# Attention and feed-forward on one core: folded weights stored in three transfers a tile, the third chunk's first unit loaded earlier, and folds, norms and global scores in other slots

## The chip, the cores and the metric

The kernel runs on one core of one Trainium2 chip. The metric is the time of one execution in device microseconds. The engines are TensorE (PE, with PEld for its weight loads), VectorE (DVE), ScalarE (ACT), GpSimd (POOL) and SyncE (SP), whose queue issues nearly all transfers (DMA).

## The reference, cut to what matters

Eight batches of eight heads: 512 local positions that attend to a window of 32 on each side and to 32 global ones, and 32 global positions that attend to everything. The result goes through an RMS norm and a gated feed-forward.

```python
s_ll = np.where(np.abs(pos[:, None] - pos[None, :]) <= 32, s_ll, -1e9)
out_l = sm(concat([s_lg, s_ll])) @ concat([v_g, v_l])     # local
out_g = sm(s_g) @ v_all                                   # global
xn = x / sqrt(mean(x * x) + 1e-6) * rms_g                 # x: 4608 x 512
return silu(xn @ w_gate) * (xn @ w_val) @ w_out           # 512 -> 1536 -> 512
```

## The kernel before

**Chunks and layers.** A chunk is the 512 local rows of one batch; chunk 8 is the 256 global rows of all. "Layer c" is the feed-forward of chunk c. While TensorE does layer c, the attention of chunk c+1 runs between its matmuls. Chunk 0, its layer and the attention of chunk 1 are written out by hand in a string `ORDER`, one token for each step (`J0 j0 u0`: the parts of fold 0; `o0`: a result of chunk 0; `U1.0` to `Y1.3`: the norm of chunk 1). Every step goes onto its engines' queues in the order of the program, and each queue runs in order.

**Slots.** From layer 1 on, one loop goes over the slots of a layer. Layer 1 has 72: 48 of products (`p`, six matmuls each, L1205) and 24 of outputs (`po`, L1266). Layers 2 to 7 are paired: seven products of halves take the place of eight, with sums and differences of weights, 42 slots of twelve matmuls (`pq`, L1108), then 24 of outputs. In each slot the program writes the slot's matmuls, then whatever attention steps are due, at most one with TensorE, then the evictions, then folds and fetches.

**Attention steps.** Chunk c has two local units, c.0 and c.1 (L loads q and k, V loads v, S the scores, M and N half a softmax each on VectorE, E and F the exponentials on ScalarE, D the division on GpSimd, T a transpose `et<-e` on VectorE, A and B the values `a<-et,v`, X and Y their eviction and squares), and from chunk 2 on a global unit between them (GL, GV loads, GS scores, GM, GN softmax, GT transposes, GA values, GD, GX). Each step names earlier steps and a distance in slots. `FIRST`, `UNIT` say from which slot a unit may begin, `LG` and `GG` hold distances: `LG[0]` is 4 slots from L to S in chunk 2, `GG[0]` 4 slots from GL to GS. A comes two slots behind the last of four T.

**Norms.** `NORM` and `NORMS` say how many slots before the end of a layer the norm of the next chunk is issued: squares, sums, all, and the halves (`ht`, `xh`, `xl`: high and low 16-bit parts that the first products of the next layer read).

**Folds.** For the paired layers the 12 weight tiles are folded once: `sums` adds high and low parts and makes four combinations in five VectorE additions (L1054 to L1058), `high` casts (ScalarE), `low` subtracts (VectorE, L155 through a helper), `store` writes the tile's quarters and combinations to a buffer `wd` in DRAM. Folds 0 to 2 stand in `ORDER`, fold 3+i in layer 1 at slots `FOLD*i`, +2, +3 and +5, with `FOLD` 8. `fetch` reads a pair's weights back for each paired layer (`wt<-wd`).

**Buffers.** The four banks `pa` of PSUM are shared by all attention steps and by the norm of chunk 1. Fold tiles, global keys, queries and values, and `ht` share six buffers `st`.

## Time and profile before

| | |
|---|---|
| median of 3 runs | 949.93 us (949.13 to 951.41) |
| the profiled execution | 949.54 us, its span 947.5 us |
| TensorE busy | 900.5 us, 95% of the span |
| VectorE, ScalarE, GpSimd busy | 635.3, 496.2, 254.2 us |
| mean granted TensorE clock | 0.980 |
| DMA queue 1 | 73824 packets, 171.41 MB, 54.8% of 16 engines |

Layer 1 begins at 170.9 us and layer 2 at 289.8; the paired layers that follow take about 100 us each; the last layer begins at 896.7. The profile lists for each engine how long it was busy, whom it waited for, and the granted clock of TensorE in any window.

### The profile page before, as it was taken

The page shows a single profiled execution, that of the slowest core. Times are in us where ns is not written, and L with a number is a line of the kernel's source. Part 1 is how long each engine was busy: PE and PEld are TensorE (multiplying, and loading weights), DVE is VectorE, ACT ScalarE, POOL GpSimd, SP SyncE. Part 2 cuts the span into 40 slices and gives each one's busy share as a digit, 9 for nine tenths or more (in the row PEclk, how much of TensorE's full clock was granted, in tenths as well). Part 3 has the DMA queues.
Part 4 walks back from the last instruction along what each step waited for, and adds up shares of the span by engine and source line. Part 5 has one row for each costly group of instructions (what it writes and reads, how often), then busy time and mean ns, then how long its engine had stood idle before and what let it go on. Part 6 is the DMA issues. An engine that isn't in the chain of part 4 may idle for free.

```text
span 947.5 us, 26480 instructions
## 1 busy us (share of the span) xinstructions
PE 900.5 (95%) x11028; PEld 615.5 (65%) x11028; DVE 635.3 (67%) x1603; ACT 496.2 (52%) x1232; POOL 254.2 (27%) x219
## 2 busy tenths in 40 slices
PE   6489899899998999999999999999999999999998
PEld 4344455544455886588747884688568865876584
DVE  6999987677767677656784679467756774655231
ACT  6999992444534573455553564357345732443131
POOL 0000000042323343323532353235333432233020
PEclk9699999999997999999999999999999999999999
DMA  9972430795449955195707762585438532787000
GB/s 351 406 277 87 158 117 2 239 266 158 147 150 312 290 184 194 48 301 192 245 36 218 250 211 108 165 283 180 159 123 300 182 102 86 234 266 236 34 1 22
DMA packets 74374, 173.41 MB, mean 183 GB/s; under 512 B 7568, under 2 KB 26256, under 8 KB 74256
## 3 DMA queue, kind: packets, MB, share of 16 engines
q1 hardware_dynamic: 73824, 171.41, 54.8%
q8 instruction: 86, 1.41, 0.6%
q10 hardware_dynamic: 432, 0.33, 0.1%
q14 instruction: 32, 0.26, 0.1%
HBM read 150.21 MB, written 21.50 MB: 181 GB/s over the span
## 4 chain that ended last, share of the span: by engine, by line
PE 80%; DMA 8%; DVE 7%; ACT 2%; issue 1%; SPq 1%; POOL 0%; ACTq 0%; DVEq 0%; POOLq 0%
PE pq L1108 35%; PE po L1266 22%; PE p L1205 9%; PE a L707 4%; PE po L1333 3%; PE s L664 3%; DMA k<-in_qk_dram 2%; DMA k<-in_qkb_dram 1%; DMA v<-in_vw_dram 1%; DMA wr<-in_w_in_dram 1%; DMA wt<-wd 1%; PE gs L780 1%; PE ga L837 1%; DMA gkq<-in_gkq_dram 1%; PE gt L823 1%
## 5 line engine op out<-in xcount | busy, mean ns | idle before, releaser
L1108 PEld LDWEIGHTS <-wt 128*128 128x128 f16 x3024 | 293.5, 98 | 46.0 <-issue 8.7
L1266 PE MATMUL po<-wo,h 128*128 128x512 f16 x1080 | 236.8, 379 | 0.5 <-POOL h L157 0.5
L1108 PE MATMUL pq<-xh,wt 128*128 128x256 f16 x1152 | 204.0, 274 | 0.5 <-issue 0.5
L1266 PEld LDWEIGHTS <-h 128*128 128x128 f16 x1080 | 105.0, 98 | 124.8 <-POOL h L157 1.0
L157 POOL TENSOR_TENSOR h<-t,h 128x512 f16<-128x512 f32 (+1 forms) x90 | 101.7, 1135 | 280.2 <-ACT h L1248 244.8
L1108 PE MATMUL pq<-ht,wt 128*128 128x256 f16 x1296 | 157.0, 273 | 3.9 <-DVE ht L155 2.1
L1108 PE MATMUL pq<-xl,wt 128*128 128x256 f16 x576 | 157.9, 274 | 0.0
L1205 PE MATMUL p<-xh,wf 128*128 128x512 f16 x384 | 120.4, 386 | 6.9 <-DVE t L1302 6.6
L1205 PEld LDWEIGHTS <-wf 128*128 128x128 f16 x576 | 56.2, 99 | 75.7 <-issue 14.4
L1140 POOL TENSOR_TENSOR s<-s,s 128x512 f32<-128x512 f32 x36 | 48.6, 1350 | 190.7 <-ACT s L1137 115.1
L626 ACT ACTIVATE e<-e,sm 128x128 f32<-128x128 f32 x192 | 75.1, 392 | 40.9 <-DVE sm L612 40.9
L641 POOL TENSOR_TENSOR e<-e,sm 128x512 f32<-128x512 f32 x48 | 50.2, 1047 | 124.5 <-DVE sm L640 121.4
L1170 ACT CAST h<-t 128x512 f16<-128x512 f32 x72 | 44.3, 616 | 58.6 <-DVE t L1162 58.0
L1162 DVE SCALAR_TENSOR_TENSOR t<-t,c_h,v 128x512 f32<-128x512 f32 x72 | 74.5, 1042 | 0.0
L1205 PE MATMUL p<-xl,wf 128*128 128x512 f16 x192 | 73.9, 385 | 0.0
L1126 DVE TENSOR_TENSOR v<-pq,s 128x512 f32<-128x512 f32 x72 | 49.6, 689 | 31.1 <-PE pq L1108 30.5
L1151 ACT ACTIVATE t<-u,half_inv 128x512 f32<-128x512 f32 x72 | 48.1, 715 | 27.6 <-DVE u L1126 19.4
L612 DVE CUSTOM_DVE_ANT_0 e<-s,maskb 128x128 f32<-128x128 f32 x192 | 45.8, 279 | 12.6 <-PE s L664 12.6
L1133 ACT COPY s<-pq 128x512 f32<-128x512 f32 x36 | 20.8, 578 | 63.2 <-PE pq L1108 63.1
L1139 DVE TENSOR_TENSOR s<-pq,s 128x512 f32<-128x512 f32 x36 | 24.8, 688 | 42.9 <-PE pq L1108 21.9
L1126 DVE TENSOR_TENSOR u<-pq,s 128x512 f32<-128x512 f32 x36 | 24.9, 692 | 38.9 <-PE pq L1108 15.4
L1158 DVE SCALAR_TENSOR_TENSOR t<-t,u 128x512 f32<-128x512 f32 x72 | 46.9, 680 | 0.0
(352 smaller groups left out, 1284.8 us busy)
## 6 DMA issues: line engine op xcount, KB each, us to landing
wt<-wd SPq DMA_DIRECT2D x114, 512.0 KB, 4.7
wr<-in_w_in_dram SPq DMA_DIRECT2D x24, 512.0 KB, 9.8
wt<-wd SPq DMA_DIRECT2D x48, 256.0 KB, 4.8
k<-in_qkb_dram SPq DMA_DIRECT2D x24, 448.0 KB, 6.2
gkq<-in_gkq_dram SPq DMA_DIRECT2D x16, 576.0 KB, 6.9
out_dram<-o SPq DMA_DIRECT2D x34, 256.0 KB, 2.0
v<-in_vb_dram SPq DMA_DIRECT2D x24, 352.0 KB, 7.2
v<-in_vw_dram SPq DMA_DIRECT2D x16, 512.0 KB, 9.6
```

Of the source, the lines that this page charges most:

```text
L157: nc.gpsimd.tensor_tensor(dst, a, b, ALU.subtract)
L612: nc.vector.tensor_tensor_reduce(out=e[:, g, :], in0=ps[:, g * P : (g + 1) * P], in1=late["mask"][:, m * P : (m + 1) * P], scale=-0.125, s ...
L626: nc.scalar.activation(e[:, g, :], e[:, g, :], AF.Exp, bias=sm[:, 0, j + g : j + g + 1], scale=-1.0, accum_out=sm[:, 1, j + g : j + g + 1],)
L641: nc.gpsimd.tensor_tensor(e, e, r.unsqueeze(2).to_broadcast([P, 4, P]), ALU.mult)
L1108: nc.tensor.matmul(ps[:, j * HT : (j + 1) * HT], w[:, j, i, k * P : (k + 1) * P], x[:, k * HT : (k + 1) * HT], start=first, stop=(p in end ...
L1126: nc.vector.tensor_tensor(o, ps, x.rearrange("p (j n) -> p j n", j=2), ALU.add)
L1140: nc.gpsimd.tensor_tensor(s(6), s(6), s(1), ALU.add)
L1151: nc.scalar.activation(t, st["u"][:, j, :], AF.Tanh, scale=half_inv[:, f : f + 1])
L1158: nc.vector.scalar_tensor_tensor(t, t, 1.0, u, ALU.add, ALU.mult)
L1162: nc.vector.scalar_tensor_tensor(t, t, c_h[:, f : f + 1], st["v"][:, j, :], ALU.mult, ALU.mult)
L1205: nc.tensor.matmul(ps[:, :n], rows[:, a, o : o + P], ch[z][k][:, :n], start=(k == 0 and i == 0), stop=(k == NK - 1 and i == 2),)
L1266: nc.tensor.matmul(ps[0], ch["h", f][:, a, j * P : (j + 1) * P], wo[f][:, z, :], start=(f == 0 and q == 0), stop=(f == NF - 1 and q == 2),)
```

## The change

1. A new step `G` in `ORDER`, ahead of fold 0, issues the loads of unit 2.0; its scores may follow in slot 0 of layer 1 (before: loads in slot 0, scores in slot 4).
2. `LG[0]` is no longer used: unit 2.1 has eight slots from L to S. `FIRST` lets global unit 0 begin at slot 14 and unit 2.1 at 22 (19 and 31).
3. `GG[0]`: six slots from a global unit's loads to its scores, in all layers.
4. `FOLD` 6: folds 3 to 11 begin at slots 0, 6, ... 48 (0, 8, ... 64).
5. `NORM`: the norm of chunk 2 is issued 4 to 5 slots earlier in layer 1, that of chunk 8 5, 7, 7 and 10 slots later in layer 7.
6. `wd` has another order of its eight parts, such that a fold is stored by three transfers and a pair's tile for a layer is fetched by one transfer in all cases, two of three full ones in two runs a partition.

```diff
-d16 A6 O2.0 X6 C7.0 C7.1 Q6 A7 a17 Z6 O2.1 X7 d17 Q7 O2.2 Z7 J0 j0 u0 O2.3 N1.0 N1.1 N1.2 N1.3
+d16 A6 O2.0 X6 C7.0 C7.1 Q6 A7 a17 Z6 O2.1 X7 d17 Q7 O2.2 Z7 G J0 j0 u0 O2.3 N1.0 N1.1 N1.2
...
-    GG = (4, 5, 4, 3)
-    NORM = {1: (16, 15, 13, 11)}
+    GG = (6, 5, 4, 3)
+    NORM = {1: (20, 19, 17, 16)}
     NORMS = (22, 21, 19, 17)
-    FIRST = (0, 19, 31)
+    FIRST = (0, 14, 22)
+    NORM[B - 1] = (17, 15, 12, 7)
-    FOLD = 8
+    FOLD = 6
...
-            ("S", scores, 1, [("L", LG[0] if c == EARLY else LG[1]), ("^Y", 1)]),
+            ("S", scores, 1, [("L", LG[1]), ("^Y", 1)]),
...
-            for q, o in ((0, 1), (1, 4), (3, 6), (2, 7)):
-                nc.sync.dma_start(to[:, o], wf[f][:, :, q * HT : (q + 1) * HT])
-            for q, o, n in ((0, 0, 1), (1, 2, 2), (3, 5, 1)):
-                nc.sync.dma_start(to[:, o : o + n], st["d"][:, q : q + n])
+            for a in range(2):
+                w = wf[f][:, a, :].rearrange("p (q n) -> p q n", q=4)
+                nc.sync.dma_start(to[:, 1::2, a, :], w)
+            nc.sync.dma_start(to[:, 0::2], st["d"])
...
-        ops = [(0, 2 * i, 2)] if i < 3 else [(0, 6, 1)]
+        o, d, n = ((0, 1, 2), (2, 2, 2), (3, 3, 2), (7, 1, 1))[i]
         if c == B:
-            ops = ([(0, 1, 1), (1, 4, 1)], [(0, 6, 2)])[i]
-        for to, o, n in ops:
-            nc.sync.dma_start(t[:, to : to + n], wd[g][:, o : o + n])
+            o, d, n = ((1, 2, 2), (5, 2, 2))[i]
+        nc.sync.dma_start(t[:, :n], wd[g][:, o : o + d * (n - 1) + 1 : d])
...
+    def first_loads():
+        for st in todo[:2]:
+            issue(st)
+            st["at"] = -LG[1]
+    job["G"] = first_loads
```

SP's queue at the end of chunk 0, before (`out_dram<-o`: the four results of chunk 0; `maskb` to `v`: the loads of unit 2.0):

```order
L1347 DMA out_dram<-o_2147 128x512
L1347 DMA out_dram<-o_2155 128x512
L1347 DMA out_dram<-o_2173 128x512
L1347 DMA out_dram<-o_2191 128x512
L586 DMA maskb<-in_maskb_dram 128x768
L587 DMA same<-in_eyes_dram 128x128
L591 DMA q_2217<-in_qkb_dram 128x512
L593 DMA k_2219<-in_qkb_dram 128x896
```

and now:

```order
L587 DMA maskb<-in_maskb_dram 128x768
L588 DMA same<-in_eyes_dram 128x128
L592 DMA q_2039<-in_qkb_dram 128x512
L594 DMA k_2041<-in_qkb_dram 128x896
L592 DMA q_2043<-in_qkb_dram 128x512
L594 DMA k_2045<-in_qkb_dram 128x896
L602 DMA v_2047<-in_vb_dram 128x704
L602 DMA v_2049<-in_vb_dram 128x704
L1347 DMA out_dram<-o_2162 128x512
L1347 DMA out_dram<-o_2170 128x512
L1347 DMA out_dram<-o_2188 128x512
L1347 DMA out_dram<-o_2206 128x512
```

The loads have moved in front of the four results.

VectorE in layer 1, ahead of the values of unit 2.1, before (`et<-e`: its last two transposes; `wq<-wf` and `ws`: the additions of fold 9; `t`: evictions of products):

```order
L646 STREAM_TRANSPOSE et_3010<-e_3086 128x512
L640 RECIPROCAL sm_2941<-sm_2941 128x4
L1236 SCALAR_TENSOR_TENSOR t_3164<-t_3164,p_11_3144 128x512
L646 STREAM_TRANSPOSE et_3011<-e_3123 128x512
L1245 SCALAR_TENSOR_TENSOR t_3164<-t_3164,c_h,p_11_3174 128x512
L1054 TENSOR_TENSOR wq_3206<-wf_1291 128x1024
L1055 TENSOR_TENSOR ws_3207<-wq_3206 128x256
```

and now (the additions are those of fold 10):

```order
L647 STREAM_TRANSPOSE et_2961<-e_3034 128x512
L641 RECIPROCAL sm_2892<-sm_2892 128x4
L1236 SCALAR_TENSOR_TENSOR t_3111<-t_3111,p_10_3091 128x512
L1054 TENSOR_TENSOR wq_3125<-wf_1335 128x1024
L1055 TENSOR_TENSOR ws_3126<-wq_3125 128x256
L1056 TENSOR_TENSOR ws_3126<-ws_3126,wq_3125 128x256
L1057 TENSOR_TENSOR ws_3126<-wq_3125 128x256
L1058 TENSOR_TENSOR ws_3126<-wq_3125,ws_3126 128x256
L647 STREAM_TRANSPOSE et_2962<-e_3071 128x512
```

The last transpose has moved behind a fold's additions.

VectorE at the end of layer 1, before (`h_2`, `ht`, `xl`: halves of the norm of chunk 2; `wq<-wf`, `ws`: fold 11; `sm`, the next row: softmax of unit 3.0):

```order
L999 TENSOR_TENSOR h_2_3595<-x_2_3336,x_0_2680 128x512
L1054 TENSOR_TENSOR wq_3598<-wf_1386 128x1024
L1055 TENSOR_TENSOR ws_3599<-wq_3598 128x256
L1056 TENSOR_TENSOR ws_3599<-ws_3599,wq_3598 128x256
L1057 TENSOR_TENSOR ws_3599<-wq_3598 128x256
L1058 TENSOR_TENSOR ws_3599<-wq_3598,ws_3599 128x256
L640 RECIPROCAL sm_3376<-sm_3376 128x4
L612 ISA e_3615,sm_3376<-s_3380,maskb 128x128
```

and now (`o`: a result of layer 1):

```order
L1000 TENSOR_TENSOR h_2_3504<-x_2_3289,x_0_2627 128x512
L1279 TENSOR_SCALAR o_3507<-po_3351,kk 128x512
L647 STREAM_TRANSPOSE et_3427<-e_3435 128x512
L641 RECIPROCAL sm_3358<-sm_3358 128x4
L613 ISA e_3533,sm_3358<-s_3360,maskb 128x128
```

Fold 11 has moved away from between `h_2` and `ht`, which is made from it.

## The prediction

> **What bounds the kernel now.** I read the page's first table and chain first, then TensorE's (PE's) waits, then the timeline of each engine around each wait. First the page: share of the span and, last, the chain by engine.

> ```profile
> PE 900.5 (95%) x11028; PEld 615.5 (65%) x11028; DVE 635.3 (67%) x1603; ACT 496.2 (52%) x1232; POOL 254.2 (27%) x219
> PE 80%; DMA 8%; DVE 7%; ACT 2%; issue 1%; SPq 1%; POOL 0%; ACTq 0%; DVEq 0%; POOLq 0%
> ```

> TensorE is busy 95% and carries 80% of the chain, and the change takes no matmul away. So only TensorE's waits can be won, and the matmuls that run on a lowered clock after a wait. This is who was waited for, by line (us in total, times, longest):

> ```profile
> PE s L664 <- DMA k<-in_qkb_dram: 3.3, 2, 2.0
> PE a L707 <- DVE et L646: 2.3, 1, 2.3
> PE pq L1108 <- DVE ht L155: 2.1, 1, 2.1
> PE a L707 <- issue: 1.9, 1, 1.9
> PE gs L780 <- DMA gkq<-in_gkq_dram: 1.7, 1, 1.7
> PE po L1266 <- POOL h L157: 0.5, 1, 0.5
> ```

> These six are 11.8 us of idle time, all at places that the change touches; the waits left out here lie nearly all in the first chunk, whose order it leaves alone. A slot, the unit in which the program places its steps, is six matmuls in layer 1 and twelve half as wide in a paired layer (chain rows):

> ```profile
> 373.39 1.30 PE po L1266 x6
> 331.66 1.31 PE pq L1108 x12
> ```

> **The change, part by part.** *Loads of unit 2.0 ahead of the results of chunk 0.* The sync queue (SP) issues in order, and its rows show why the first scores of layer 1 wait (start, duration):

> ```profile
> 146.71 1.10 PE L536 MATMUL a<-v,pt 128*32 128x64 f32 x64
> 168.40 3.64 SPq L1347 DMA_DIRECT2D out_dram<-o  x4
> 179.51 0.42 PE L664 MATMUL s<-k,q 64*32 64x128 f32 x8 [1.99 <-DMA k<-in_qkb_dram]
> 181.21 3.23 PE L664 MATMUL s<-k,q 64*32 64x128 f32 x120 [1.27 <-DMA k<-in_qkb_dram]
> ...
> 332.90 2.05 PE L664 MATMUL s<-k,q 64*32 64x128 f32 x128
> ```

> The four results of chunk 0 hold the loads back until 172.0, and the scores end at 184.44. TensorE had been free since 179.51 - 1.99 = 177.5, and undisturbed scores last 2.05 (layer 2's), so 6.9 - 2.0 = 4.9 us are lost. In the new order the loads wait only for their buffers, which the last values of chunk 0 free at 147.8, some 24 us before the scores, now in slot 0. Those need the four PSUM banks that the norm of chunk 1 has just used; VectorE (DVE) empties the last one here:

> ```profile
> 172.25 0.74 DVE L903 SCALAR_TENSOR_TENSOR xl<-x13t,gvec,xh 128x512 f16<-128x512 f32 x1
> ```

> It ends at 172.99; the scores would begin near 172.2 and come to that bank a microsecond later. Cost of the new wait: 0 to 0.8, I take 0.2. Gain 4.7. Behind it unit 2.0's softmax starts earlier beside fold 3, and its values stay 14 slots behind its scores (4 to 18 before, 0 to 14 now). I net that wait at 0, with -0.5 and +1.5 as ends.

> *Unit 2.1's loads 9 slots ahead of its scores instead of 4.* Its scores lasted 2.54 while the keys landed, against the 2.05 above: gain 0.5, at worst 0.

> ```profile
> 235.46 2.54 PE L664 MATMUL s<-k,q 64*32 64x128 f32 x128
> ```

> *Folds every 6 slots instead of 8.* This is the part that can cost. VectorE's busy time in the stretch of layer 1 up to unit 2.1's last values:

> ```profile
> 172.00:262.00 90.00, 64.41 (x161) 0.96 0.67 205
> ```

> By then seven of the nine folds are done; now it will be eight, some 4 us more (five additions at 2.72 by the starts below, a subtraction at 1.2). The stretch loses four slots of 1.30 and about 5 us of waits. So 68.5 us of work go into 80: 86% where it was 72%. At one place the order itself gets worse. Unit 2.1's last transpose (T3) stood ahead of a fold's additions, now it stands behind fold 10's. Before, on VectorE, and the values on TensorE:

> ```profile
> 244.53 1.22 DVE L1054 TENSOR_TENSOR wq<-wf 128x1024 f32<-128x1024 f16 x1
> 247.25 0.70 DVE L646 STREAM_TRANSPOSE et<-e 128x512 f32<-128x512 f32 x1
> ...
> 254.30 0.71 DVE L646 STREAM_TRANSPOSE et<-e 128x512 f32<-128x512 f32 x1 [0.40 <-POOL e L641]
> ...
> 256.28 1.54 PE L707 MATMUL a<-et,v 32*64 32x256 f32 x80
> ```

> A fold's additions hold VectorE from 244.53 to 247.25, 2.72 us. T3 ended at 255.0, 1.3 us before the values. It now ends 2.72 - 0.40 later (the wait for POOL is filled), and up to 0.8 more where POOL slows the additions or ACT starts later; the values stay 14 slots behind the scores. That is a new wait of 1.0 to 1.9, plus what VectorE is behind by. I take 2.0, with 0 and 2.8 as ends. Behind the waiting values stands only the next slot of products.

> Does such a wait also lower the clock? This window stands right behind the "issue" wait of 1.9 us (its numbers: length, busy, granted clock, DMA share, GB/s):

> ```profile
> 210.40:214.80 4.40, 4.40 (x17) 0.61 0.97 265
> ```

> 1.9 us idle was followed by 4.40 us at 0.61, a loss of 1.7. Behind the 1.7 us wait for gkq (below) the matmuls kept their pace. So the clock term for a wait of 2.0 is 0 or 1.7; I leave it at 0 and put 1.7 into the upper end. [...]

> *Folds and the norm out of the end of layer 1.* Around the change of layers TensorE waits twice, and VectorE is the reason:

> ```profile
> 287.62 1.22 DVE L1054 TENSOR_TENSOR wq<-wf 128x1024 f32<-128x1024 f16 x1
> 291.25 0.93 DVE L155 TENSOR_TENSOR ht<-h,ht 128x512 f16<-128x512 f32 x1
> 293.30 1.21 DVE L155 TENSOR_TENSOR wq<-ws,wq 128x1024 f16<-128x1024 f32 x1
> 296.54 0.70 DVE L646 STREAM_TRANSPOSE et<-e 128x512 f32<-128x512 f32 x1
> ...
> 292.23 1.70 PE L1108 MATMUL pq<-ht,wt 128*128 128x256 f16 x11 [2.13 <-DVE ht L155]
> 297.30 2.44 PE L707 MATMUL a<-et,v 32*64 32x256 f32 x78 [2.32 <-DVE et L646]
> ...
> 292.30:295.00 2.70, 2.67 (x13) 0.65 0.97 302
> 297.30:303.10 5.80, 5.80 (x95) 0.50 0.78 231
> ```

> Fold 11's additions (2.72) stand right ahead of ht's low half, its subtraction (1.2) ahead of T3 of unit 3.0, and VectorE has no gap there. Idle: 2.13 + 2.32. Slow clock: 2.70 x 0.35 + 5.80 x 0.50 = 0.9 + 2.9. Together 8.3. Now both last folds are over by slot 53, the norm starts 4 to 5 slots (5 to 6.5 us) earlier against a wait of 2.1, and unit 3.0's chain loses 2.72 + 2 x 1.2 of foreign work against a wait of 2.3. Both waits go, and with them the clock loss: gain 8.3. If one of them stays, half goes: 4.2.

> *Global units' scores 6 slots behind their loads instead of 4.* In layer 7 two scores wait for gkq; beside them an undisturbed one:

> ```profile
> 310.76 1.20 PE L780 MATMUL gs<-gkq 64*32 64x272 f32 x32
> 805.82 1.75 PE L780 MATMUL gs<-gkq 64*32 64x272 f32 x32
> 836.37 0.66 PE L780 MATMUL gs<-gkq 64*32 64x272 f32 x8
> 838.72 1.12 PE L780 MATMUL gs<-gkq 64*32 64x272 f32 x24 [1.69 <-DMA gkq<-in_gkq_dram]
> ```

> Lost: 0.6, and 839.84 - 836.37 - 1.1 = 2.4. Two slots of a paired layer are 2.6 us, so scores that would begin at 839.0 find the tile that landed at 838.7. Gain 3.0; 1.5 if it lands later. In layers 2 to 6 the transposed result (GX) moves behind the next unit's scores and takes the bank that the first two half softmaxes free; in layer 2 those end at 335.6, and TensorE gets there one slot behind the scores, at 334.95 + 1.31 = 336.3, so 0, at worst 0.6 in each of five layers.

> ```profile
> 335.34 0.28 DVE L612 CUSTOM_DVE_ANT_0 e<-s,maskb 128x128 f32<-128x128 f32 x1
> ```

> *The last norm later.* Its POOL additions kept h back for the 0.5 us of the last wait listed above: gain 0.5. It now ends 7 slots (9.1 us) later than here, and it was ready 17 us before the last layer's products:

> ```profile
> 878.34 0.75 DVE L155 TENSOR_TENSOR xl<-xg,xh 128x256 f16<-128x256 f32 x2
> 896.72 31.44 PE p L1205 x288
> ```

> *Three store transfers instead of seven, strided fetches.* Same bytes in the same runs of 512 B and 1 KB; fetches in two runs instead of one. SP issues three transfers where it issued seven, of the same rows in all, so it is busy no longer than before. No TensorE row waits for wt or for a store, so 0 on the path. The cover is that a fold's buffer is needed again 7 slots (9.1 us) behind its store; stores land in 4.0 us (last number, a median).

> ```profile
> wd<-wf SPq DMA_DIRECT2D x48, 128.0 KB, 4.0
> ```

> *The "issue" wait* of 1.9 (3.6 with its slow clock) has no cause that the profile names. It fell among small matmuls, and the DMA share right behind it is 0.97. The new order puts the same values two slots behind the loads of the same global unit, so I keep it: 0, with 3.6 gained or a second one of 3.6 as ends.

> **Sum.** -4.7 - 0.5 + 0 + 2.0 - 8.3 - 3.0 - 0.5 + 0 = -15.0. The profiled execution took 949.54 (span 947.5, 2.0 around it), 0.04% under the median of 949.93. 949.54 - 15.0 = 934.5.

> **The rivals.** (a) The "issue" wait goes too: 934.5 - 3.6 = 930.9. For it: the loads of unit 2.0 leave the crowded start of layer 1. Against: the stores there are as many.

> (b) VectorE becomes the bound of layer 1. At 86% it falls behind, unit 2.0's values wait 1.5, unit 2.1's 2.8 with a clock loss of 1.7, and its scores 0.8 for the bank that GD frees behind fold 8: 1.5 + 0.8 + 1.7 + 0.8 = 4.8 more, 939.3. For it: T3's place. Against: in the stretch up to 262 no TensorE row waits for VectorE today.

> (c) One wait between layers 1 and 2 stays, because unit 3.0's chain still has the same 17 slots: 934.5 + 4.2 = 938.7.

> (d) Slower: the stores of three transfers land too late. Folds 8, 10 and 11 reuse a tile whose store was issued 7 slots (9.1 us) earlier. What lands later holds VectorE, and at 86% that goes on to TensorE, three times. To end above 951.4 it needs 16.9 us, 5.6 each: landing after 14.7 us, against 4.0 above. (e) No change: the loads are not early, because SP stands still, and VectorE's waits come back elsewhere: 949.

> **Numbers.** Forecast 0.45, own range 932 to 937.5; (a) 0.22, (b) 0.16, (c) 0.09, (d) 0.05, (e) 0.03. A measurement of this kernel can tell about 0.2% (1.9 us) from no change. Faster holds all but the last two: 0.92; same 0.03; slower 0.05. The range of 928 to 941 takes in (a) to (c) with some 2 us around them; it leaves out (d), (e) and mixtures of (b) with (c).

> **What would show it.** Right: scores of unit 2.0 undisturbed near 172 to 174.4; no wait and a granted clock of 1.00 at the start of layer 2; gs of 1.1 in layer 7; a wait of a L707 for et of about 2 us near 240. Wrong: PE waits in layer 1 for VectorE of more than 4 us, a clock below 1 there, or VectorE waiting for a DMA at L1054.

## The result, and the profile after

The new kernel takes 934.77 us, the one before 949.53 (medians of six runs each). The ratio is 0.9845, 95% interval 0.982 to 0.987: 14.7 us faster, where 15.0 was forecast (934.5). One of the six runs took 3231.63 us, is disturbed and is left out of the ratio; the other five lie between 932.32 and 936.85, with a median of 934.41. The profiled execution is the fastest of them, 932.32 us (span 930.2), so its trace, read against the 949.54 of before, shows 17.2 us, and 2.5 of that are the luck of this execution.

The page: busy time and the chain by engine.

```profile
PE 893.9 (96%) x11028; PEld 612.2 (66%) x11028; DVE 634.0 (68%) x1603; ACT 495.4 (53%) x1232; POOL 253.8 (27%) x219
...
PE 82%; DVE 8%; DMA 4%; ACT 3%; issue 1%; POOL 1%; ACTq 0%; DVEq 0%; POOLq 0%
```

TensorE has the same matmuls and is 6.6 us less busy, since fewer ran on a lowered clock (a mean of 0.989 against 0.980). Its waits outside the first chunk (us in total, times, longest):

```profile
PE a L708 <- DVE et L647: 2.5, 2, 2.1
PE pq L1108 <- issue: 0.9, 1, 0.9
PE a L708 <- issue: 0.2, 1, 0.2
```

Of the six waits listed before, together 11.8 us, four are gone: for the keys, for ht, for gkq and for h. The values' wait for et is another one, in another unit, and the values' "issue" wait is gone from its place. The first scores of unit 2.0, those of unit 2.1, and the second pair in layer 7 (start, duration):

```profile
140.88 0.42 SPq L592 DMA_DIRECT2D q<-in_qkb_dram  x1
...
168.38 3.64 SPq L1347 DMA_DIRECT2D out_dram<-o  x4
...
172.12 2.06 PE L665 MATMUL s<-k,q 64*32 64x128 f32 x128
...
172.23 0.74 DVE L904 SCALAR_TENSOR_TENSOR xl<-x13t,gvec,xh 128x512 f16<-128x512 f32 x1
...
221.96 2.06 PE L665 MATMUL s<-k,q 64*32 64x128 f32 x128
...
824.03 1.70 PE L781 MATMUL gs<-gkq 64*32 64x272 f32 x32
```

The loads leave 27 us ahead of the results, the scores begin at once and pay nothing for the bank that VectorE empties last. What VectorE does ahead of the values of unit 2.1, and the values on TensorE:

```profile
240.37 1.53 DVE L1054 TENSOR_TENSOR wq<-wf 128x1024 f32<-128x1024 f16 x1
241.94 1.26 DVE L1055 TENSOR_TENSOR ws<-wq 128x256 f32<-128x256 f32 x1
...
244.24 0.70 DVE L647 STREAM_TRANSPOSE et<-e 128x512 f32<-128x512 f32 x1
...
242.29 0.64 PE L708 MATMUL a<-et,v 32*64 32x256 f32 x2
245.00 1.52 PE L708 MATMUL a<-et,v 32*64 32x256 f32 x78 [2.06 <-DVE et L647]
```

This is the wait that was forecast at 2.0. From 242.29 to 246.52 the 80 values take 4.23, where 1.54 is undisturbed (quoted in the prediction): 2.7 are lost, since the two matmuls ahead of the wait, 0.64 in the trace, are shown too long (the 78 behind it take 1.52). The change of layers, its first product and its window (length, busy, then clock, DMA share, GB/s at the end), and the stretch for which 68.5 us of VectorE's work were forecast:

```profile
283.84 0.64 PE L708 MATMUL a<-et,v 32*64 32x256 f32 x2
284.88 1.52 PE L708 MATMUL a<-et,v 32*64 32x256 f32 x78 [0.41 <-DVE et L647]
286.34 1.48 PE L1108 MATMUL pq<-ht,wt 128*128 128x256 f16 x12
...
172.00:252.00 80.00, 77.92 (x1022) 39.76 (x1022) 68.53 (x168) 42.36 (x120) 25.94 (x21) 1.00 0.70 211
285.00:300.00 15.00, 14.79 (x282) 12.91 (x282) 5.75 (x10) 5.47 (x10) 2.54 (x2) 1.00 1.00 312
```

The time by layer, from the first product of one to that of the next in the two timelines (us):

| layer | before | after | difference |
|---|---|---|---|
| 1 | 119.08 | 115.61 | -3.5 |
| 2 | 110.38 | 100.48 | -9.9 |
| 3 and 4 | 202.60 | 201.50 | -1.1 |
| 5 and 6 | 196.37 | 196.50 | +0.1 |
| 7 | 97.38 | 94.29 | -3.1 |

Unit 3.0's first values now stand in layer 1 instead of layer 2. They take 2.5 us there (283.84 to 286.34), 1.0 more than undisturbed. So the rest of layer 1 gained 6.0, and the rest of layer 2 9.9 - 1.5 = 8.4.

### The profile page after: what moved, and what is told of

It is laid out like the page before. It is cut to its first block, busy times and chain, and to the rows that moved or that the text cites. A ratio compares the mean times of both kernels' runs of the same rounds, so it can differ in the third digit from the quotient of the medians.

```text
span 930.2 us, 26398 instructions
## 1 busy us (share of the span) xinstructions
PE 893.9 (96%) x11028; PEld 612.2 (66%) x11028; DVE 634.0 (68%) x1603; ACT 495.4 (53%) x1232; POOL 253.8 (27%) x219
## 3 DMA queue, kind: packets, MB, share of 16 engines
q8 instruction: 86, 1.41, 0.6%
## 4 chain that ended last, share of the span: by engine, by line
PE 82%; DVE 8%; DMA 4%; ACT 3%; issue 1%; POOL 1%; ACTq 0%; DVEq 0%; POOLq 0%
PE pq L1108 36%; PE po L1266 23%; PE p L1205 9%; PE a L708 4%; PE po L1333 3%; PE s L665 3%; DMA k<-in_qk_dram 2%; DMA v<-in_vw_dram 1%; DMA wr<-in_w_in_dram 1%; PE ga L838 1%; PE gs L781 1%; PE gt L824 1%; DVE wf L373 1%; ACT wr L272 1%; DVE t L1302 1%
## 5 line engine op out<-in xcount | busy, mean ns | idle before, releaser
L1108 PEld LDWEIGHTS <-wt 128*128 128x128 f16 x3024 | 292.6, 98 | 40.9 <-issue 5.3
L1266 PE MATMUL po<-wo,h 128*128 128x512 f16 x1080 | 236.2, 379 | 0.0
L1108 PE MATMUL pq<-xh,wt 128*128 128x256 f16 x1152 | 204.3, 273 | 0.0
L1266 PEld LDWEIGHTS <-h 128*128 128x128 f16 x1080 | 105.2, 98 | 123.9 <-issue 1.0
L1108 PE MATMUL pq<-xl,wt 128*128 128x256 f16 x576 | 157.0, 273 | 0.0
L1108 PE MATMUL pq<-ht,wt 128*128 128x256 f16 x1296 | 155.6, 273 | 0.9 <-issue 0.9
L1205 PE MATMUL p<-xh,wf 128*128 128x512 f16 x384 | 119.4, 382 | 6.9 <-DVE t L1302 6.3
L1205 PEld LDWEIGHTS <-wf 128*128 128x128 f16 x576 | 55.9, 99 | 74.4 <-issue 12.4
L1205 PE MATMUL p<-xl,wf 128*128 128x512 f16 x192 | 73.5, 383 | 0.0
L1162 DVE SCALAR_TENSOR_TENSOR t<-t,c_h,v 128x512 f32<-128x512 f32 x72 | 70.7, 989 | 0.0
```

The lines of the kernel that those rows point to most:

```text
L1108: nc.tensor.matmul(ps[:, j * HT : (j + 1) * HT], w[:, j, i, k * P : (k + 1) * P], x[:, k * HT : (k + 1) * HT], start=first, stop=(p in end ...
L1162: nc.vector.scalar_tensor_tensor(t, t, c_h[:, f : f + 1], st["v"][:, j, :], ALU.mult, ALU.mult)
L1205: nc.tensor.matmul(ps[:, :n], rows[:, a, o : o + P], ch[z][k][:, :n], start=(k == 0 and i == 0), stop=(k == NK - 1 and i == 2),)
L1266: nc.tensor.matmul(ps[0], ch["h", f][:, a, j * P : (j + 1) * P], wo[f][:, z, :], start=(f == 0 and q == 0), stop=(f == NF - 1 and q == 2),)
```

## The experiments

My theory was the sum on record: each part of the change takes away its own wait. The rivals were that another part carries the gain, or that the "issue" wait goes as well. No run undoes `FIRST` or the eight slots of unit 2.1 alone. Each kernel was timed beside the kernel before; unless named, its ratio is to be read against the 0.9845 of the new kernel.

**The loads alone, on the kernel before.**

```diff
-d16 A6 O2.0 X6 C7.0 C7.1 Q6 A7 a17 Z6 O2.1 X7 d17 Q7 O2.2 Z7 J0 j0 u0 O2.3 N1.0 N1.1 N1.2 N1.3
+d16 A6 O2.0 X6 C7.0 C7.1 Q6 A7 a17 Z6 O2.1 X7 d17 Q7 O2.2 Z7 G J0 j0 u0 O2.3 N1.0 N1.1 N1.2 N1.3
...
+            issue(st)
+            st["at"] = -LG[0]
+
+    job["G"] = first_loads
```

> The kernel before, with step G alone: the loads of unit 2.0 ahead of the four results, its scores in slot 0. All other steps stay where they were before. My theory: the loads behind the results cost 4.7 to 5.3 us, so this runs 5 us faster than before (944.5), its first scores last 2.05 with no wait for the keys, and the two waits between layers 1 and 2 (2.1 and 2.3, with their lowered clock) and those for gkq stay. Theory of the issue wait: if the wait of 1.9 us for nothing at 208.5 us came from the crowded start of layer 1, it goes too, and with it the slow matmuls behind it, together 3.6 more: 941. If it hangs on what else stands there, it stays.

941.73 us, ratio 0.9925 (0.990 to 0.9949): 7.1 us faster. In layer 1 only this wait of TensorE for another engine is left ahead of its last slots:

```profile
193.32 1.52 PE L707 MATMUL a<-et,v 32*64 32x256 f32 x78 [0.55 <-DVE et L646]
```

Layer 1 is 8.7 us shorter: some 5 are the scores', the rest is the "issue" wait with its slow matmuls, which is gone. So what rival (a) foresaw came, but not for its reason: the second part of the same values ran from 197.47 us on without a wait, with a DMA share of 0.99 from 197 to 199. The last section has the cause. The two waits between the layers (2.1 and 3.1) and that for gkq (1.6) stayed.

**Folds every 8 slots again.**

```diff
-    FOLD = 6
+    FOLD = 8
```

> The new kernel with the folds every 8 slots again, all else new (norm of chunk 2 early, loads early). Fold 11's additions then stand at slot 64, its subtraction at 67, ahead of the last transpose of unit 3.0 in slot 69; fold 10's no longer stand ahead of the last transpose of unit 2.1. My theory: the wait of 2.06 at 245 us goes, and unit 3.0's values wait for VectorE by 2 to 4 us more than the 0.4 of now, with up to 2.9 of slow clock behind it: between equal to the new kernel and 5 us slower, 2 slower likeliest (936.5). Rival: the earlier norm alone removed the waits between the layers; then there is no wait there and this is 2 us faster than the new kernel (932.5).

941.43 us, ratio 0.9927 (0.9903 to 0.9952): about 7 us slower than the new kernel, beyond what I expected. The chain around the end of layer 1 (start, us, what):

```profile
284.25 2.10 DVE wq L1054
...
287.51 0.42 DVE ws L1058
...
290.26 0.57 DVE wq L156
...
291.76 0.71 DVE et L647
...
292.51 2.44 PE a L708 x63
```

Fold 11's additions and its subtraction stand ahead of two transposes of unit 3.0. TensorE waits 5.0 and then 2.7 for them (the first is named an issue, but it ends within 0.1 us of the end of the transpose before), and 290 to 294 us had a granted clock of 0.50. The additions took 3.7 here, not 2.72.

**The norm of chunk 2 as late as before.**

```diff
-    NORM = {1: (20, 19, 17, 16)}
+    NORM = {1: (16, 15, 13, 11)}
```

> The new kernel with the norm of chunk 2 as late as before (16, 15, 13 and 11 slots before the end of layer 1), folds every 6 slots. My theory: the folds' work on VectorE made the waits between the layers, the norm has room to be late; ht was 2.1 late with fold 11's additions of 2.7 ahead of it, and is in time without them: 0 to 1 us slower than the new kernel. Rival: the norm's place carries the gain; then products of layer 2 wait for ht by 2 us or more and with the slow clock behind it this is 3 to 8 us slower than the new kernel.

937.55 us, ratio 0.9883 (0.9859 to 0.9907): some 3 us slower, though the two intervals just overlap; the profile shows where. The place is neither theory's. No product waits for ht; the norm's own work on VectorE holds up unit 3.0's last transpose. Two rows of the chain, and the values of unit 3.0:

```profile
286.71 1.10 DVE xl L156
...
287.96 1.64 DVE h L1000
...
290.28 1.71 PE a L708 x54
```

The wait is 3.4 us. So both parts were needed between the layers: VectorE must be rid of the last fold and of the norm, or unit 3.0 pays for whichever is left.

**Four slots from a global unit's loads to its scores.**

```diff
-    GG = (6, 5, 4, 3)
+    GG = (4, 5, 4, 3)
```

> The new kernel with four slots from a global unit's loads to its scores instead of six. My theory: in layer 7 two scores wait again for gkq, 0.6 and 2.4 us lost, 3.0 in all; in layers 2 to 6 nothing changes, or up to 0.5 is gained in layer 1, where the scores now come at 203.7 us and last 1.5 instead of 1.1. So 2.5 to 3 us slower than the new kernel. Rival: the waits for gkq came from what the queue carried at that time, the transfers of the weights in their old form, and not from the two slots; then it is equal to the new kernel and gs in layer 7 lasts 1.1.

943.71 us, ratio 0.9941 (0.9924 to 0.9958): 9 us slower, three times what I expected. Layer 7 shows 1.5 of it, with the wait for gkq back at 1.0. Layer 1 shows 6.8, at a place that I had not looked at:

```profile
204.22 0.42 DVE L721 COPY x<-a 128x256 f32<-128x256 f32 x1
...
204.69 0.69 PE L781 MATMUL gs<-gkq 64*32 64x272 f32 x14 [2.34 <-DVE x L721]
...
263.43 1.91 PE L1266 MATMUL po<-wo,h 128*128 128x512 f16 x7 [2.31 <-POOL h L158]
```

With global unit 0 let in at slot 14, four slots put its scores two slots behind unit 2.0's last values, ahead of the eviction that empties their bank, and that eviction stood behind a fold's additions. The loads were in time. The other wait, for POOL's h, was followed by 4.4 us at a clock of 0.65; why h came late there isn't shown.

**Stores and fetches in their old form.**

```diff
+            for q, o in ((0, 1), (1, 4), (3, 6), (2, 7)):
+                nc.sync.dma_start(to[:, o], wf[f][:, :, q * HT : (q + 1) * HT])
...
+        ops = [(0, 2 * i, 2)] if i < 3 else [(0, 6, 1)]
```

> The new kernel with the stores and fetches of before: seven transfers store a fold, and a pair's tile is fetched from adjacent parts. Everything else is new. My theory: no engine waits for a store or for a fetched tile, so the time is that of the new kernel (within 1 us of 934.6). Rival: the new form makes the transfers shorter or fewer, and with them go waits for nothing that the profile names and waits for gkq; then this is 2 us or more slower than the new kernel, with such waits of over 1 us in layers 1 to 4 or at gs in layer 7.

934.34 us, ratio 0.9849 (0.9825 to 0.9874): the time of the new kernel. Its profile (940.77, the slowest of its six runs) has an "issue" wait of 2.7 behind the change of layers, but the other runs don't bear it out (933.33 to 935.97). In layer 7, gs lasts 1.15 and 1.76, as in the new kernel. The part is worth 0, as forecast.

**The last norm as early as before.**

```diff
-    NORM[B - 1] = (17, 15, 12, 7)
```

> The new kernel with the norm of chunk 8 as early as before in layer 7. My theory: one wait of outputs for POOL's h of 0.5 us comes back near 860 us and nothing else: 0.5 us slower than the new kernel, less than this measurement can tell, so the profile decides. Rival: no such wait, since layer 7 now runs without the waits for gkq that shifted it: equal in the profile too.

936.1 us, ratio 0.9858 (0.9839 to 0.9876). The wait is back, at its length of before:

```profile
PE po L1265 <- POOL h L157: 0.5, 1, 0.5
```

**Folds 10 and 11 two slots later.**

```diff
-                        if k == FOLD * i + d:
+                        if k == FOLD * i + d + 2 * (i >= 7):
```

> The new kernel with folds 10 and 11 two slots later (from slots 44 and 50 instead of 42 and 48). The additions of fold 10 then stand behind the last transpose of unit 2.1 on VectorE. My theory: the wait of 2.06 for et at 245 us goes, nothing comes instead, since fold 11 is over by slot 55 and the halves of the norm begin at slot 56: 2 us faster than the new kernel, and up to 1.7 more where slow matmuls follow that wait (932.5). Rival: VectorE has no room left, and the wait comes back at the next thing that TensorE needs of it (outputs for h, or unit 3.0's values): equal to the new kernel.

929.95 us, ratio 0.980 (0.9781 to 0.9819): 4 to 5 us faster than the new kernel, and the fastest here. The last transpose of unit 2.1 now runs ahead of the additions:

```profile
240.65 0.71 DVE L647 STREAM_TRANSPOSE et<-e 128x512 f32<-128x512 f32 x1 [0.40 <-POOL e L642]
241.91 1.21 DVE L1054 TENSOR_TENSOR wq<-wf 128x1024 f32<-128x1024 f16 x1
...
242.09 1.54 PE L708 MATMUL a<-et,v 32*64 32x256 f32 x80
```

No wait, and none in its place. Layer 1 is 2.74 us shorter than in the new kernel's profile, the 2.7 that the wait cost there.

**Fold 10's additions made twice.**

```diff
-            nc.vector.tensor_tensor(t[0], wf[f][:, 0, :], wf[f][:, 1, :], ALU.add)
+            for _ in range(2 if f == 10 else 1):
+                nc.vector.tensor_tensor(t[0], wf[f][:, 0, :], wf[f][:, 1, :], ALU.add)
...
```

> The new kernel with the five additions of fold 10 made twice, with the same sums as result. They stand ahead of unit 2.1's last transpose and took 3.87 us in the profile of the new kernel (2.72 elsewhere). My theory: that stretch is on the path, so the wait of 2.06 grows to 4.8 to 5.9, and after so long a wait the clock is lowered in every run, 1.7 to 2 us more: 4.5 to 6 us slower than the new kernel (940). Rival: VectorE's later idle time takes part of it up, or the wait was for POOL's or ScalarE's part of the chain: then the wait grows by less than 2 and the time by less than 2.

939.34 us, ratio 0.9885 (0.9867 to 0.9903): 4 us slower, a little under the 4.5 to 6 expected. The waits, and the window behind the long one:

```profile
PE a L708 <- DVE et L647: 5.3, 2, 4.9
...
248.95:253.35 4.40, 4.40 (x83) 2.72 (x84) 2.51 (x3) 2.15 (x3) 1.15 (x1) 0.50 0.01 4
```

The second set took 2.7 us, the wait grew by 2.85 (2.06 to 4.91): VectorE's work there stands on the path one for one, and the clock behind it was 0.50, a loss of 4.40 x 0.50 = 2.2. Set against the mean loss of 1.0 that the new kernel has there (next section), 2.85 + 2.2 - 1.0 gives the 4.

**The kernel before and the new one once more.**

> The kernel before, unchanged, for a second profile of it. My theory: the waits that the profile names an issue are late instructions of TensorE: they fall at the same place of its instruction stream in every run (after 4254 matmuls and weight loads, 10113, 12919), since the page shows a queue of instructions with 86 transfers of 16.4 KB, and are as long as the transfer of the next 16 KB is late. So a wait of 1 to 3 us for nothing stands again in unit 2.0's values, after 4254 instructions, and the other waits of this kernel are there again too. Rival: the wait of 1.9 us at 210 us was chance, and it is not there.

> The new kernel, unchanged, for a second profile of it beside the others. My theory: the wait of 2.06 for et in unit 2.1's values is there again with the same length, since it hangs on the order alone; what varies is the clock behind it: 1.00 in the first profile, 0.59 to 0.64 in three kernels with the same wait. So 933 to 936 us, with the slow clock where it is near the upper end. No wait of over 0.3 us in unit 2.0's values.

The kernel before took 951.12 us. Its waits stand where they stood; the one in unit 2.0's values is 1.7 long. The new kernel: 935.71 us, ratio 0.9856 (0.9842 to 0.9871), and the wait of 2.06 is there, with no slow matmul behind it.

**Fetches at the end of layer 1 spread out** (with folds 10 and 11 later).

```diff
-                if -12 <= k - total < -4:
+                if k - total in range(-20, -4, 2):
```

> The new kernel with folds 10 and 11 two slots later, and the eight fetches of weights at the end of layer 1 in every second slot from the 20th before the end on, instead of in eight slots in a row from the 12th. My theory: the wait for nothing in unit 3.0's values just behind the change of layers (0.2 to 2.7 us, after 6289 instructions in all kernels with this order) is a late transfer of instructions while the data transfers fill the engines (DMA share 0.98 to 1.05); spread out, they leave room and it goes: 0 to 1 us faster than with the folds alone (929.4). Rival: the wait stays, as the global unit's loads at the start of layer 2 fill the engines anyway, or the fetches now hold up fold 11's stores: equal to 929.95 or slower.

930.33 us, ratio 0.9798 (0.9782 to 0.9814). The "issue" wait behind the change of layers is gone, as expected, and the time is equal: it was 0.27 us.

**Layer 4's fetches made twice** (with folds 10 and 11 later; the second one writes the same tile again).

```diff
+        for _ in range(2 if c == 4 else 1):
             nc.sync.dma_start(t[:, :n], wd[g][:, o : o + d * (n - 1) + 1 : d])
```

> The new kernel with folds 10 and 11 two slots later, and each fetch of the weights of layer 4 (issued while layer 3 runs) issued twice, into the same tile. The transfers of layer 3 double. My theory: the waits for nothing in layer 3, which fall at multiples of 256 TensorE instructions where the scores use up 256 instructions in 2 us (0.65 to 2.5 us after 10120 instructions, in all profiles so far), grow where the data transfers fill the engines: the one at 10120 becomes 2 us or more, a second may appear at a later place in layer 3; with slow clock behind it 2 to 6 us slower than 929.95. Rival: the wait has another cause than the transfers, and stays at 0.6 to 1: no difference, unless products wait for wt, which would show as a wait for a DMA.

985.74 us, ratio 1.0388 (1.0368 to 1.0409), 56 us slower, but not in the way expected. The fetches run ahead by some eight tiles, so the doubled ones began behind the place that I meant to load, and the wait there was 0.3. TensorE was stopped by the fetches themselves and by the loads that stand behind them:

```profile
PE pq L1109 <- DMA wt<-wd: 14.0, 6, 5.3
PE s L665 <- DMA k<-in_qkb_dram: 12.7, 5, 8.3
PE ga L838 <- DMA gv<-in_gv_dram: 8.2, 1, 8.2
```

For the cause of the "issue" waits this run says little: one of 0.97 us stands at 448.23, in layer 3, where no other profile has one, but the DMA share in the 4.2 us up to it was only 0.47.

## Why the prediction was right, point by point

**The first scores.** Forecast -4.7 and -0.5 for unit 2.1. Both scores last 2.06 and wait for nothing; with the loads alone, layer 1 lost about 5 that are theirs. Right, and the new wait for the bank (0.2) did not come.

**Unit 2.0's values.** Forecast 0, with ends -0.5 and +1.5. The loads alone brought a wait of 0.55, the new kernel has none. Right.

**The new wait for et.** Forecast 2.0; 2.06 by the waits in both profiles of the new kernel, 2.7 by the values' own times. The working was less good than the number: the additions took 3.87 instead of 2.72 (GpSimd's addition for h ran beside them, from 240.78 to 242.91; the second one took 1.26 there, and 0.42 at 245.78 in the kernel before, with GpSimd idle), and the transpose's slack was 0.7 instead of 1.3 (with folds 10 and 11 later it ends at 241.36, the values begin at 242.09), so the working gives 3.87 - 0.40 - 0.73 = 2.7, which is what the values lost. Its price was mis-sized too: taking it away gave 4 to 5 us in the medians, not 2. The step that was wrong there is "the clock term for a wait of 2.0 is 0 or 1.7; I leave it at 0". Four kernels, in five profiles, have this wait with the length of 2.06. The 4.4 us behind it, in the new kernel's two profiles, then with the late norm, the old stores and the early last norm:

```profile
245.00:249.40 4.40, 4.40 (x112) 2.64 (x120) 2.65 (x4) 2.15 (x3) 1.16 (x1) 1.00 0.37 144
245.76:250.16 4.40, 4.40 (x112) 2.64 (x120) 2.65 (x4) 2.15 (x3) 1.16 (x1) 1.00 0.24 94
245.81:250.21 4.40, 4.40 (x85) 2.33 (x86) 2.51 (x3) 2.15 (x3) 1.15 (x1) 0.65 0.26 102
245.30:249.70 4.40, 4.40 (x85) 2.73 (x86) 2.50 (x3) 2.15 (x3) 1.16 (x1) 0.61 0.30 115
245.62:250.02 4.40, 4.40 (x85) 2.40 (x86) 2.50 (x3) 2.15 (x3) 1.15 (x1) 0.62 0.29 113
```

Two at full clock, three at 0.61 to 0.65: 4.40 x 0.35 to 0.39 = 1.5 to 1.7 us, three times in five, 1.0 as a mean. The term was 0 or 1.7, and it is now one, now the other, by where the wait falls (last section). The new kernel was lucky in both its profiles (932.32 and 934.64 us). With 1.0 the wait costs 3.7; the rest of the 4 to 5 that the medians show lies within their intervals.

**Between the layers.** Forecast -8.3 for both waits and the clock. Layer 2 lost 8.4 beside the values that moved out of it; 1.0 came back with the wait inside them, so -7.4. The page's clock there is 1.00. Right, with the folds and the norm both needed, which the two kernels with one of them undone show (7 and 3 us). Rival (c), a wait of 2 us that stays, did not come.

**gs.** Forecast -3.0 in layer 7 and 0 elsewhere. Layer 7 lost 3.1 with the 0.5 of the last norm in it, so about 2.6; the second scores still take 1.70. Elsewhere "0" was right for the change as a whole, but I missed what the two slots do in layer 1, where undoing them costs 6.8. It did not count in the sum, because there the earlier `FIRST` and the longer distance came together; that follows from the order of the steps, no run shows it.

**The last norm, the stores, the fetches.** Forecast -0.5 and 0. The wait of 0.54 comes back when the norm does; the old stores change nothing. The norm's sums moved by six slots (21 to 15), not by the seven that the list of the change gives; its last parts are ready at 871.3, 7.8 us before the last layer, so nothing hangs on it.

**The "issue" wait.** Forecast 0, with 3.6 as the end. This term was wrong: the wait is gone in both profiles of the new kernel and with the loads alone. The step that failed is "The new order puts the same values two slots behind the loads of the same global unit, so I keep it": it took the neighbouring transfers for the cause, when the wait stands on a grid in the instruction stream and ends 1.62 us behind the landing of a transfer of instructions (last section). The term is -1.7 to -3.6: the two profiles of before have the wait at 1.86 and 1.74, and only the first has slow matmuls behind it.

So the sum of 15.0 came out with two errors that cancel: this wait gone, by 1.7 to 3.6, and the wait for et dearer than 2.0, by 0.7 in the profile and by 2 to 3 in the medians. That the sum lies so close to the 14.7 measured is luck to that extent; the other terms are right in their mechanism. In layers 3 and 4 another 1.1 went in the profile, from "issue" waits that vary (1.74 and 0.5 before, 0.92 after; 2.02 and 0.50, 1.47 and 0.32 in the second profiles); that is no gain of the change.

VectorE's load was forecast at 68.5 us in 80 and is 68.53, and rival (b) did not come: at 86% busy only the one place where the order is wrong made TensorE wait.

## What to carry to other kernels

A wait is priced by what stands ahead of the late instruction on its own engine: read those rows, and the place of the next consumer, before the busy share; 86% was harmless, 3.9 us of additions in the wrong place cost 4 to 5. Where two edits clear the same stretch of one engine, or one makes room that the other uses, undoing either shows more than its own term, so parts don't add up. And a move that wins 15 us is worth a second look at the one wait that it makes: two slots' shift of two folds won 4 to 5 more.

## What the runs showed of the hardware that I had not expected

**"Issue" waits sit on a grid.** Before its instruction at 210.37 us TensorE had executed these many matmuls and weight loads in the kernel before (counts behind the busy times of PE and PEld), likewise at 436.93, and the same in its second profile and in the new kernel:

```profile
0.00:210.35 210.35, 176.23 (x2127) 100.16 (x2127) 177.12 (x494) 158.56 (x357) 12.39 (x13) 0.94 0.60 211
0.00:436.90 436.90, 396.46 (x5056) 247.28 (x5057) 331.71 (x881) 266.82 (x645) 85.52 (x73) 0.96 0.62 206
...
0.00:211.75 211.75, 177.84 (x2127) 100.68 (x2127) 177.21 (x494) 158.82 (x357) 12.39 (x13) 0.94 0.60 209
...
0.00:202.00 202.00, 173.23 (x2125) 97.81 (x2126) 175.75 (x494) 157.98 (x357) 10.98 (x12) 0.95 0.64 221
0.00:423.30 423.30, 390.93 (x5060) 243.98 (x5060) 331.79 (x881) 266.13 (x644) 85.48 (x73) 0.98 0.64 213
q8 instruction: 86, 1.41, 0.6%
```

The two together are 4254 and 10113, 4254 again, and, in the new kernel, 4251 (it does instruction 4254 at 202.28) and 10120. The page's queue q8 moved instructions in 86 transfers, 1.41 MB, 16.4 KB each; 22056 matmuls and weight loads over 86 are 256 for each. In units of 256 the counts are 16.62, 39.50 and 39.53; others were 2.70, 3.70, 24.57, 28.56, 42.53, 50.46 to 50.50 and 60.48. They lie in the middle of a unit, not at its ends as I had it ahead of the doubled fetches, with a slow drift from 0.70 to 0.46, in all 14 profiles but for two waits: the one in the kernel with eight-slot folds that was VectorE's, and one amid the doubled fetches. So the waits fall whole multiples of about 256 matmuls and weight loads apart, in stretches of many small matmuls or just behind them. That TensorE goes over to its next 16.4 KB of instructions there is my reading.

The traces also hold q8's transfers one by one. Before the wait that ended at 210.37 one started at 207.82 and landed at 208.75; this is q8 in the window 207.8 to 208.8 of the kernel before:

```profile
q8 instruction: 1, 0.02, 5.8%
```

All 53 waits on the grid end 1.21 to 1.62 us behind the landing of such a transfer; for the two others the last landing was 15 us back or more. I take from this timing that TensorE waits there for its next instructions, and that their transfer starts late; it does not run longer than elsewhere (0.88 to 1.20 us, where the median over the kernel before is 1.06). Full DMA engines are neither needed for such a wait nor enough: the DMA share in the 3.2 us up to the end of this one was 0.68, and 0.52 in the second profile, and while the transfer ran ahead of the wait of 0.50 that ended at 540.01 (537.68 to 538.63) it was 0.12; in the new kernel the same step falls at 202 us, among large products, with a share of 0.99 from 198 to 204, the transfer lands 2.7 us ahead of it, and there is no wait. What sets the start of such a transfer isn't shown. The waits last 0.2 to 2.7 us.

**The clock behind one and the same wait varies, with a grid in time.** 2.06 us of idle time was followed by 1.00 or by 0.61 to 0.65; two of the three kernels with the slow clock have the new kernel's order up to there (the third, with the old stores, has other transfers). The granted clock of a trace changes only at instants that lie 3.41 us or whole multiples of it apart (in the one of before, around layer 1, it is 0.50 from 180.47 to 183.88, from 211.19 to 214.60 and from 293.11 to 303.35), and the profiles differ in how the wait falls on these steps. The two steps (length, then TensorE's busy time; the clock is the third number from the end) around the wait in the new kernel, where it is cut in two, and in the one with the late norm, where it lies within one:

```profile
240.60:244.01 3.41, 2.34 (x11) 0.77 (x8) 3.34 (x5) 0.00 (x0) 2.31 (x2) 1.00 1.02 275
244.01:247.42 3.41, 2.42 (x83) 1.79 (x84) 1.78 (x4) 1.81 (x3) 1.12 (x1) 1.00 0.70 257
...
243.69:247.10 3.41, 1.34 (x79) 1.25 (x78) 2.66 (x6) 0.68 (x2) 0.04 (x1) 1.00 0.93 352
247.10:250.51 3.41, 3.41 (x23) 1.23 (x12) 1.93 (x2) 1.48 (x2) 1.15 (x1) 0.50 0.03 8
```
